# A linear-attention and expert-MLP kernel: numerators in three steps, another order of the first units, and queries rounded by a DMA

## The chip, the core and the metric

The kernel runs on one NeuronCore of a Trainium2 chip. A NeuronCore has five engines that run side by side, each through its own list of instructions in order: TensorE (PE, matrix products into PSUM), VectorE (DVE), ScalarE (ACT), GpSimd (POOL) and SyncE (SP, which here only issues DMAs). They wait for one another by semaphores. The metric is the device time of one execution in microseconds (us).

## The reference

Three stages follow one another, all in float32:

```python
# 1. linear attention, q, k, v: (2, 8, 576, 64), w_phi: (64, 128)
proj = x @ w_phi                                   # for x = q and x = k
proj = proj - max(abs(proj), axis=-1)
phi  = concat([exp(proj), exp(-proj)])             # 256 features
kv   = k_p.T @ v;  z = sum(k_p, axis=seq)
out  = (q_p @ kv) / (q_p @ z + 1e-6)               # numerator / denominator
# 2. x (1152, 512):  x = ((x @ w_a) * (x @ w_b)) @ w_out        # 1536 inner columns
# 3. four experts:   out = sum_e p_e * (relu(x @ w1[e]) @ w2[e])   # 1024 inner columns each
```

## The kernel before

**Split operands.** Most float32 matrix products are made of three products of rounded parts (type fp32r): high by high, high by low, low by high. So each operand has a high part (the value rounded) and a low part (the value minus the high part). `two_parts` makes the pair: a copy with rounding on ScalarE (L84) and a subtraction on another engine, mostly GpSimd (L85). Some products (`kv`, `num`, the transposes `rt`) run in plain float32; the profile counts each of those matmuls twice.

**The attention loop.** The loop over `slot` has 36 items, 18 of keys (slots 0 to 17) and 18 of queries (slots 18 to 35), then ten slots more. An item is 256 columns of k or q: two tiles of 128 tokens by two heads. In a slot:

- `split_x(slot + 3)` makes the two parts `xp` of the item three slots ahead from `xraw`, which holds three items and is loaded by SP (L100);
- `stage_proj(slot)` multiplies six times with w_phi (`pj`, L165 to L167); VectorE takes the maximum (`mx`, L170) and subtracts it (`r`, L172);
- for keys, three slots later, `stage_kv` accumulates `kv` (L199);
- for queries, four slots later, `stage_rt` transposes `r` on TensorE (`rt`, L219) and ScalarE writes the exponentials `qp` (L237);
- when all `qp` of two pairs of heads (a half of a batch; there are four halves) are there, `stage_num` runs in the next slot: three groups of matmuls in a row (denominator, then two numerators, `num`, L265), each into a tile of the pool `nd` with two buffers. ScalarE copies the denominator (`den`, L272), VectorE turns it into reciprocals (L279 to L284) a slot later and multiplies the numerators (`x`, L289), and `stage_xparts` makes the parts `xh` (ScalarE, L295) and `xl` (GpSimd, L296).

`pj`, `rt` and, later, `ab` share the four PSUM buffers of the pool `u`: TensorE can't go on with a new tile before VectorE or ScalarE has read an old one.

**The weights.** The weights of stage 2 are prepared beside this by tasks of a list: `begin` (two ScalarE instructions, `m` and `rn`), `middle` (three VectorE instructions, L369 to L375, one GpSimd addition `wx`, L378, and the next load `raw` by SP) and `parts` (`w`, ScalarE L84 and GpSimd L85). `prep(n)` issues the next n tasks. Before, slots 10 and 14 issue three each, and every slot from 20 on issues one.

**Stage 2.** A unit `unit_ab(j, tp)` treats 256 inner columns for batch `tp` in eight chunks of twelve matmuls (`ab`, L608 to L610); it writes its result `hh` once per four chunks. Its eight products with w_out (`o1`, six matmuls each) go to a queue and run during later units; `free_hh(tp)` runs those of the same batch that are still queued before `hh` is written again. The first unit, (0, 0), is the `fill`: its chunks are issued in the last attention slots, two each in slots 40, 42, 43 and 44 (`FILL`), while batch 1 is still in attention. Then `order` lists the units: (0, 0), (0, 1), (1, 0), (1, 1), (2, 0) and so on.

Of the kernel before, what the change touches and what calls it, by code (L numbers as in the profile page):

```python
# [47 lines left out]
def tile_linear_attention_then_mlps(ctx, tc, qT, kT, v, w_phi, wab, wout, w12, probs, out):  # L48
# [25 lines left out]
    with tc.manual_schedule():  # L74
# [16 lines left out]
        def load_chunk(n):  # L91
# [9 lines left out]
            xraw[n] = t  # L101

        def split_x(i, eng):
            n, c = i // 3, i % 3 * 256
            if c == 0:
                xpart[n] = [r_p.tile([128, NC], F32R, tag=f"xp{k}", name="xp", bufs=2) for k in range(2)]
            hi, lo = (t[:, c:c + 256] for t in xpart[n])
            if i == 0:
                nc.vector.tensor_copy(hi, xraw[n][:, 0:256])
                nc.vector.tensor_tensor(out=lo, in0=xraw[n][:, 0:256], in1=hi.bitcast(F32), op=ALU.subtract)  # L110
# [34 lines left out]
        seq = tiles_of_batch()  # L145
        items = []
        for kind in "kq":
# [10 lines left out]
        def stage_proj(i):  # L158
            kind, b, g, ts_ = items[i]
            ps = u_p.tile([128, 2, 2, 128], F32, tag="u", name="pj")  # L160
            for j in range(2):
                c = i % 3 * 256 + j * 128
                hi, lo = (t[:, c:c + 128] for t in xpart[i // 3])
# [49 lines left out]
        def stage_rt(i):  # L213
# [6 lines left out]
            for t in ts_:  # L220
                for p in ([t[0]] if t[0] != "m" else t[1:]):
                    if (b, p) not in qp_t:
                        qp_t[b, p] = q_p.tile([128, 2, 2, S], F32, tag="qp", name="qp", bufs=3)
            done = []
# [27 lines left out]

        def stage_num(b, half):
            pairs = [(b, 2 * half + k) for k in range(2)]
            qp = [qp_t.pop(bp) for bp in pairs]
            den = q_p.tile([128, 2, HT], F32, tag="den", name="den", bufs=1)
            x = []
            for k in range(3):
                t = nd_p.tile([128, 2, 512], F32, tag="nd", name="num")
                for i in range(2):  # L260
                    for s in range(2):
                        for n in range(4):
                            h = n % 2
                            c = 64 * (1 - h) if k == 0 else 64 * h + 32 * (k - 1)
                            nc.tensor.matmul(  # L265
                                out=t[32 * n:32 * n + 32, i, 0:HT],
                                lhsT=kvz_t[pairs[n // 2]][:, h, s, c:c + 32],
                                rhs=qp[n // 2][:, s, h, HT * i:HT * i + HT],
                                start=(s == 0), stop=(s == 1), tile_position=(0, 32 * n),
                            )  # L270
                if k == 0:
                    nc.scalar.activation(out=den, in_=t[:, :, 0:HT], func=AF.Copy, bias=1e-6)  # L272
                else:
                    x.append(t)
            return x, den

# [471 lines left out]

        NI = len(items)
        NK = NI // 2  # L750
        todo = {}
# [16 lines left out]
        FILL = [NI + 4, NI + 6, NI + 7, NI + 8]  # L768
        fill = unit_ab(0, 0)

        for slot in range(NI + 10):
            if slot < NI:
                kind, b, g, ts_ = items[slot]
                if slot + 3 < NI:
                    split_x(slot + 3, nc.gpsimd)
                stage_proj(slot)
            if slot == NK + 4:
# [11 lines left out]
            if NK <= i < NI:  # L789
                for bb, p in stage_rt(i):  # L790
                    if p % 2:
                        n = slot + (2 if i == NI - 1 else 1)
                        later(n, num, n, bb, p // 2)
            for fn, a in todo.pop(slot, []):
# [6 lines left out]
            if slot == 16:  # L801
                probabilities()
            if slot in FILL:
                for _ in range(2):
                    next(fill)
                    pos[0] += 1
            if slot in (10, 14):
                prep(3)
            if slot >= NK + 2:
                prep(1)  # L810
        assert not todo
# [78 lines left out]
```

## Time and profile before

| | |
|---|---|
| time, median of 3 runs | 735.85 us (735.56 to 736.63) |
| the profiled execution, its own time | 734.41 us |
| its span in the trace | 732.6 us |
| TensorE busy | 711.3 us, 97% |
| VectorE, ScalarE, GpSimd busy | 57%, 42%, 41% |
| share of TensorE in the chain that ended last | 92% |
| mean granted clock of TensorE | 0.998 of full speed |

The profile is of one execution. TensorE is busy nearly everywhere; its idle time is the span less its busy time, 21 us in all. The views by stretches and the waits of TensorE show where these microseconds lie; the share of busy time of the other engines over the whole span says little about the stretches in which TensorE waits for them.

### The profile page before, as it was taken

To read this page: it belongs to the slowest core of one execution; us is meant where nothing else is said; L and a number is where in the kernel's file an instruction comes from. 1 tells how busy PE (TensorE), PEld (TensorE's weight loads), DVE (VectorE), ACT (ScalarE), POOL (GpSimd) and SP (SyncE) were. 2 spreads that over 40 slices of the span, in tenths; PEclk is the share of its full clock that TensorE was granted. 3 is DMA by queue.
4 is the path that set the end of the run, shared out by engine and by line. 5 is a ranking of instruction groups with operands and counts; after the bars stand their busy time and mean duration, and the time that the engine had idled before them with its cause. 6 is when DMAs were issued, how large, how long until landed. Compare 5 with 4: busy or idle time off the path is not lost.

```text
span 732.6 us, 12645 instructions
## 1 busy us (share of the span) xinstructions
PE 711.3 (97%) x4928; PEld 652.1 (89%) x4928; DVE 419.3 (57%) x717; ACT 304.2 (42%) x626; POOL 302.9 (41%) x277
## 2 busy tenths in 40 slices
PE   7998988999999999999899999999999999999998
PEld 7996657999999999999888898988988898989896
DVE  6678796446666575363545555545455545545454
ACT  6566764554535351243553333323233323333221
POOL 3356545444434354312683425344442535343300
PEclk9999999999999999999999999999999999999999
DMA  7534211222323231022041011111111011100003
GB/s 200 148 111 125 58 59 59 82 92 87 91 83 87 78 96 30 1 58 86 2 116 30 30 57 58 30 55 33 58 40 47 30 59 58 30 29 1 1 1 129
DMA packets 49707, 46.25 MB, mean 63 GB/s; under 512 B 8304, under 2 KB 41584, under 8 KB 49648
## 3 DMA queue, kind: packets, MB, share of 16 engines
q1 hardware_dynamic: 49344, 45.26, 21.0%
q8 instruction: 38, 0.62, 0.4%
q10 hardware_dynamic: 304, 0.20, 0.1%
q14 instruction: 21, 0.17, 0.1%
HBM read 43.08 MB, written 2.36 MB: 62 GB/s over the span
## 4 chain that ended last, share of the span: by engine, by line
PE 92%; DVE 3%; ACT 3%; issue 1%; POOL 1%; DMA 0%; DVEq 0%; ACTq 0%; POOLq 0%
PE acc L682 9%; PE acc L681 9%; PE acc L680 9%; PE ab L609 7%; PE ab L610 7%; PE ab L608 7%; PE X L533 5%; PE kv L199 5%; PE X L534 5%; PE X L535 5%; PE acc L639 3%; PE acc L640 3%; PE acc L638 3%; PE num L265 3%; PE Z L534 2%; PE Z L533 2%
## 5 line engine op out<-in xcount | busy, mean ns | idle before, releaser
L696 DVE SCALAR_TENSOR_TENSOR oacc<-acc,pr,oacc 128x512 f32<-128x512 f32 (+1 forms) x136 | 101.4, 746 | 117.2 <-PE acc L682 117.2
L85 POOL TENSOR_TENSOR w<-wx,w 128x512 fp32r<-128x512 f32 x68 | 92.1, 1355 | 154.9 <-ACT w L84 154.9
L609 PE MATMUL ab<-xl,w 128*128 128x288 f32 x384 | 113.3, 295 | 2.0 <-POOL xl L296 2.0
L85 POOL TENSOR_TENSOR wc<-wt,wc 128x512 fp32r<-128x512 f32 (+1 forms) x48 | 69.8, 1483 | 109.4 <-ACT wc L84 109.4
L682 PE MATMUL acc<-w,hhb 128*128 128x512 f32 x288 | 114.1, 396 | 0.9 <-DVE hhb L657 0.9
L608 PE MATMUL ab<-xh,w 128*128 128x288 f32 x384 | 113.5, 296 | 1.2 <-ACT xh L295 1.2
L610 PE MATMUL ab<-xh,w 128*128 128x288 f32 x384 | 113.4, 295 | 0.0
L681 PE MATMUL acc<-w,hhb 128*128 128x512 f32 x288 | 113.1, 393 | 0.0
L680 PE MATMUL acc<-w,hhb 128*128 128x512 f32 x288 | 112.6, 391 | 0.0
L533 PE MATMUL X<-xc,wc 128*128 128x288 f32 x256 | 77.2, 302 | 1.4 <-ACT h L538 1.4
L534 PE MATMUL X<-xc,wc 128*128 128x288 f32 x256 | 75.8, 296 | 0.7 <-DVE xc L85 0.7
L656 ACT ACTIVATE hhb<-h 128x288 fp32r<-128x288 f32 x64 | 36.2, 566 | 96.8 <-DVE h L541 96.7
L535 PE MATMUL X<-xc,wc 128*128 128x288 f32 x256 | 75.4, 295 | 0.0
L609 PEld LDWEIGHTS ab<-xl,w 128*128 128x128 f32 x384 | 72.2, 188 | 2.2 <-POOL xl L296 2.2
L608 PEld LDWEIGHTS ab<-xh,w 128*128 128x128 f32 x384 | 72.2, 188 | 1.9 <-ACT xh L295 1.5
L378 POOL TENSOR_TENSOR wx<-wx,rn 128x512 uint32<-128x512 uint32 x36 | 46.3, 1287 | 63.1 <-DVE wx L375 63.1
L610 PEld LDWEIGHTS ab<-xh,w 128*128 128x128 f32 x384 | 72.2, 188 | 0.0
L538 ACT ACTIVATE h<-X 128x288 f32<-128x288 f32 x64 | 25.9, 405 | 104.5 <-PE X L535 104.5
L682 PEld LDWEIGHTS acc<-w,hhb 128*128 128x128 f32 x288 | 54.0, 188 | 15.6 <-DVE hhb L657 4.4
L657 DVE SCALAR_TENSOR_TENSOR hhb<-h,hhb 128x288 fp32r<-128x288 f32 x64 | 40.5, 633 | 42.2 <-ACT hhb L656 42.2
L681 PEld LDWEIGHTS acc<-w,hhb 128*128 128x128 f32 x288 | 54.0, 188 | 8.4
L680 PEld LDWEIGHTS acc<-w,hhb 128*128 128x128 f32 x288 | 54.1, 188 | 7.7
(99 smaller groups left out, 1605.8 us busy)
## 6 DMA issues: line engine op xcount, KB each, us to landing
raw<-in_wab SPq DMA_DIRECT2D x192, 64.0 KB, 2.0
wt<-in_w SPq DMA_DIRECT2D x64, 128.0 KB, 2.4
wx<-in_w SPq DMA_DIRECT2D x32, 256.0 KB, 2.9
raw<-in_wout SPq DMA_DIRECT2D x12, 512.0 KB, 3.7
xraw<-in_qT SPq DMA_DIRECT2D x6, 384.0 KB, 3.1
out<-oacc SPq DMA_DIRECT2D x8, 256.0 KB, 2.0
xraw<-in_kT SPq DMA_DIRECT2D x5, 384.0 KB, 4.2
v<-in_v SPq DMA_DIRECT2D x8, 192.0 KB, 4.4
```

The lines of the kernel that those rows point to most:

```text
L85: eng.tensor_tensor(out=lo, in0=src, in1=hi.bitcast(F32), op=ALU.subtract)
L378: nc.gpsimd.tensor_tensor(out=x, in0=x, in1=r, op=ALU.add)
L533: nc.tensor.matmul(out=ps, lhsT=whi, rhs=xhi, start=first and a == 0, stop=False, skip_group_check=True)
L534: nc.tensor.matmul(out=ps, lhsT=whi, rhs=xlo, start=False, stop=False, skip_group_check=True)
L535: nc.tensor.matmul(out=ps, lhsT=wlo, rhs=xhi, start=False, stop=a == 1, skip_group_check=True)
L608: nc.tensor.matmul(out=t, lhsT=whi, rhs=hi, start=(c == 0), stop=False)
L609: nc.tensor.matmul(out=t, lhsT=whi, rhs=lo, start=False, stop=False)
L610: nc.tensor.matmul(out=t, lhsT=wlo, rhs=hi, start=False, stop=(c == KD - 1))
L680: nc.tensor.matmul(out=acc, lhsT=hi, rhs=w[:, 0, f], start=f == 0, stop=False)
L681: nc.tensor.matmul(out=acc, lhsT=hi, rhs=w[:, 1, f], start=False, stop=False)
L682: nc.tensor.matmul(out=acc, lhsT=lo, rhs=w[:, 0, f], start=False, stop=f == 1)
L696: nc.vector.scalar_tensor_tensor(out=oc, in0=acc[:, c:c + step], scalar=sc, in1=oc, op0=ALU.mult, op1=ALU.add)
```

## The change

1. **Numerators in three steps.** The denominator's group of matmuls runs in one slot, the first numerator's in the next, the second's in the one after. `qp` gets four buffers instead of three. The last half starts one slot earlier (slot 40, not 41), and the loop has 45 slots, not 46.
2. **Order of the first units.** After (0, 0) comes (1, 0), then (0, 1) and (1, 1). The chunks of the fill stand in slots 38, 39, 40 (one each), 42 (two), 43 (one) and 44 (two).
3. **High parts of the queries by DMA.** `load_hi` lets GpSimd's queue load each query item's 256 columns a second time, straight into the fp32r tile: 18 DMAs, in slots 12 to 29, six slots ahead of their use. `split_x` then makes only the low part, on GpSimd (L124 of the new file). The tiles `xp` now hold one item each, seven buffers for high parts and four for low ones.
4. **Weight tasks.** `PREP` issues one task in each of the slots 5 to 16, in every second slot from 20 to 34, and in the slots 36 to 44.

```diff
+        def load_hi(i):
+            if NK <= i < NI:
+                xpart[i] = part_x(0)
+                c = i % 3 * 256
+                nc.gpsimd.dma_start(out=xpart[i], in_=qT[i // 3 - B * 3][:, c:c + 256])
...
+            raw = xraw[n][:, c:c + 256]
+            hi = xpart[i] if i >= NK else part_x(0)
+            lo = part_x(1)
...
+            elif i < NK:
+                two_parts(hi, lo, raw, eng)
             else:
-                two_parts(hi, lo, xraw[n][:, c:c + 256], eng)
+                eng.tensor_tensor(out=lo, in0=raw, in1=hi.bitcast(F32), op=ALU.subtract)
...
         def num(slot, b, half):
-            later(slot + 1, div, slot + 1, b, half, *stage_num(b, half))
-
-        def div(slot, b, half, x, den):
+            pairs = [(b, 2 * half + k) for k in range(2)]
+            qp = [qp_t.pop(bp) for bp in pairs]
+            kvz = [kvz_t[bp] for bp in pairs]
+            den = stage_den(stage_num(qp, kvz, 0))
+            later(slot + 1, first, slot + 1, b, half, qp, kvz, den)
+
+        def first(slot, b, half, qp, kvz, den):
+            t = stage_num(qp, kvz, 1)
             rb = stage_rc(den)
-            for k in range(2):
-                later(slot + 1 + k, scaled, slot + 1 + k, b, 2 * half + k, x[k], rb)
-
-        def scaled(slot, b, c, t, rb):
-            later(slot + 1, stage_xparts, b, c, stage_x(t, rb))
-
-
-        FILL = [NI + 4, NI + 6, NI + 7, NI + 8]
+            later(slot + 1, second, slot + 1, b, half, qp, kvz, rb, t)
+
+        def second(slot, b, half, qp, kvz, rb, t0):
+            t1 = stage_num(qp, kvz, 2)
+            later(slot + 1, stage_xparts, b, 2 * half, stage_x(t0, rb))
+            later(slot + 1, third, slot + 1, b, half, rb, t1)
+
+        def third(slot, b, half, rb, t1):
+            later(slot + 1, stage_xparts, b, 2 * half + 1, stage_x(t1, rb))
+
+
+        FILL = {NI + 2: 1, NI + 3: 1, NI + 4: 1, NI + 6: 2, NI + 7: 1, NI + 8: 2}
+        PREP = {s: 1 for s in range(5, NK - 1)} | {s: 1 for s in range(NK + 2, NI, 2)} | {s: 1 for s in range(NI, NI + 9)}
...
-        order = [(j, tp) for j in range(FP1 - 2) for tp in range(B)]
+        order = [(0, 0), (1, 0), (0, 1), (1, 1)] + [(j, tp) for j in range(2, FP1 - 2) for tp in range(B)]
```

On TensorE, where the first half of batch 0 is ready, the three groups stood in one piece before (`num`, 48 matmuls, each of which the trace counts twice); `pj` are projections, `rt` transposes:

```order
L219 MATMUL rt<-ident,r 128x128 x4
L265 MATMUL num<-qp,kvz 32x288 x48
L165 MATMUL pj<-wbp,xp 128x256
L166 MATMUL pj<-wbp,xp 128x256
L167 MATMUL pj<-wbp,xp 128x256
```

At the same place now:

```order
L232 MATMUL rt<-ident,r 128x128 x4
L273 MATMUL num<-qp,kvz 32x288 x16
L178 MATMUL pj<-wbp,xp 128x256
L179 MATMUL pj<-wbp,xp 128x256
L180 MATMUL pj<-wbp,xp 128x256
L178 MATMUL pj<-wbp,xp 128x256
L179 MATMUL pj<-wbp,xp 128x256
L180 MATMUL pj<-wbp,xp 128x256
L232 MATMUL rt<-ident,r 128x128 x4
L273 MATMUL num<-qp,kvz 32x288 x16
```

A slot's projections and transposes now stand between two groups of 16.

On GpSimd, at the end of the keys and the start of the queries, the low parts (`xp`) stood among the weight tasks (`w`, `wx`) before:

```order
L85 TENSOR_TENSOR xp<-xraw,xp 128x256 x6
L85 TENSOR_TENSOR w<-wx,w 128x512
L85 TENSOR_TENSOR xp<-xraw,xp 128x256
L378 TENSOR_TENSOR wx<-wx,rn 128x512
L85 TENSOR_TENSOR xp<-xraw,xp 128x256 x2
```

Now (L124 is a query's subtraction, L110 the DMA of a high part):

```order
L85 TENSOR_TENSOR w<-wx,w 128x512
L124 TENSOR_TENSOR xp<-xraw,xp 128x256
L110 DMA xp<-in_qT 128x256
L387 TENSOR_TENSOR wx<-wx,rn 128x512
L124 TENSOR_TENSOR xp<-xraw,xp 128x256
L110 DMA xp<-in_qT 128x256
L124 TENSOR_TENSOR xp<-xraw,xp 128x256
L110 DMA xp<-in_qT 128x256
```

Each of the subtractions in these slots has a DMA behind it in the same queue.

On TensorE, where the fill ends and the next unit begins, numbers tell the tiles apart. Before, `xh_784` was batch 0, `xh_786` batch 1, and the next unit took batch 1 with the same weights `w_565`:

```order
L608 MATMUL ab_1622<-xh_784,w_825 128x288
L609 MATMUL ab_1622<-xl_785,w_825 128x288
L610 MATMUL ab_1622<-xh_784,w_825 128x288
L608 MATMUL ab_1667<-xh_786,w_565 128x288
L609 MATMUL ab_1667<-xl_787,w_565 128x288
L610 MATMUL ab_1667<-xh_786,w_565 128x288
```

Now `xh_844` is batch 0, and the next unit stays with it:

```order
L617 MATMUL ab_1661<-xh_844,w_629 128x288
L618 MATMUL ab_1661<-xl_845,w_629 128x288
L619 MATMUL ab_1661<-xh_844,w_629 128x288
L617 MATMUL ab_1695<-xh_844,w_1410 128x288
L618 MATMUL ab_1695<-xl_845,w_1410 128x288
L619 MATMUL ab_1695<-xh_844,w_1410 128x288
```

The unit behind the fill needs other weights (`w_1410`) and no tile of batch 1.

## Rows read from the trace of the kernel before

**Rows 1.** Stretches: start:end, length, each engine's busy time (x instructions), TensorE's clock, DMA share, GB/s.
```profile
0.00:56.20 56.20, 51.83 (x448) 50.66 (x449) 39.01 (x68) 34.35 (x71) 23.35 (x34) 1.00 0.56 150
56.20:68.20 12.00, 8.72 (x70) 7.56 (x73) 11.30 (x19) 9.99 (x27) 7.00 (x9) 1.00 0.41 126
68.20:80.80 12.60, 11.31 (x136) 7.64 (x136) 9.31 (x16) 7.49 (x20) 6.50 (x8) 1.00 0.33 99
80.80:94.40 13.60, 12.29 (x143) 8.05 (x142) 11.46 (x18) 8.66 (x22) 7.75 (x8) 1.00 0.14 40
94.40:104.00 9.60, 8.30 (x108) 4.17 (x109) 9.27 (x14) 6.19 (x15) 6.76 (x5) 1.00 0.22 64
114.00:128.50 14.50, 11.29 (x83) 10.85 (x83) 8.61 (x13) 5.40 (x10) 6.21 (x5) 1.00 0.12 37
```
**Rows 2.** Waits of TensorE: us in total, times, longest.
```profile
PE rt L219 <- ACT qp L237: 2.9, 2, 1.5
PE ab L609 <- POOL xl L296: 2.0, 1, 2.0
PE ab L608 <- ACT xh L295: 1.2, 1, 1.2
```
**Rows 3.** Stretches of 10 us behind the handover to batch 1.
```profile
130.00:140.00 10.00, 10.00 (x66) 10.00 (x65) 3.35 (x7) 5.38 (x12) 3.51 (x4) 0.83 0.35 105
140.00:150.00 10.00, 10.00 (x78) 10.00 (x77) 5.64 (x10) 5.47 (x12) 5.50 (x4) 1.00 0.29 80
```
**Rows 4.** Timeline of VectorE: start, length, instruction, count, idle time before it.
```profile
58.33 0.42 DVE L369 TENSOR_SCALAR m<-m 128x512 f32<-128x512 f32 x1
...
59.91 0.68 DVE L170 TENSOR_REDUCE mx<-pj 128x4 f32<-128x512 f32 x1
...
61.30 0.68 DVE L170 TENSOR_REDUCE mx<-pj 128x4 f32<-128x512 f32 x1
...
75.10 0.69 DVE L170 TENSOR_REDUCE mx<-pj 128x4 f32<-128x512 f32 x1 [2.96 <-PE pj L167]
...
87.85 0.69 DVE L170 TENSOR_REDUCE mx<-pj 128x4 f32<-128x512 f32 x1 [1.77 <-PE pj L167]
```
**Rows 5.** Timeline of TensorE, numerators.
```profile
68.12 6.03 PE L265 MATMUL num<-qp,kvz 128*32 128x288 f32 x96
...
96.53 1.16 PE L265 MATMUL num<-qp,kvz 128*32 128x288 f32 x12 [0.49 <-ACT qp L237]
97.90 2.15 PE L265 MATMUL num<-qp,kvz 128*32 128x288 f32 x32 [0.21 <-DVE x L289]
```
**Rows 6.** Instructions on the tile xraw: duration in ns, least/median/most, first and last start.
```profile
L84 ACT ACTIVATE xp<-xraw x35: 397/402/495, 3.7 to 85.4; 128x256 fp32r<-128x256 f32 x35
L85 POOL TENSOR_TENSOR xp<-xraw,xp x33: 722/728/968, 6.4 to 88.1; 128x256 fp32r<-128x256 f32 x33
L100 SPq DMA_DIRECT2D xraw<-in_qT x6: 328/337/371, 37.6 to 68.9; - x6
L85 DVE TENSOR_TENSOR xp<-xraw,xp x2: 418/418/419, 4.7 to 5.0; 128x256 fp32r<-128x256 f32 x2
```
**Rows 7.** Timeline of SP's queue: a DMA of v in many pieces.
```profile
9.96 0.61 SPq L133 DMA_DIRECT2D v<-in_v  x1
```
**Rows 8.** Groups by form, GpSimd's weight tasks, 30 to 128.5 us: count, busy us, mean ns.
```profile
L85 POOL TENSOR_TENSOR w<-wx,w 128x512 fp32r<-128x512 f32 x10 | 13.3, 1332 | 8.4 <-ACT w L84 8.4
L378 POOL TENSOR_TENSOR wx<-wx,rn 128x512 uint32<-128x512 uint32 x10 | 12.7, 1275 | 24.2 <-DVE wx L375 24.2
```
**Rows 9.** Page, DMA issues: count, KB each, median us to landing.
```profile
xraw<-in_qT SPq DMA_DIRECT2D x6, 384.0 KB, 3.1
```
**Rows 10.** Timeline of VectorE: one instruction (L372) at two places.
```profile
94.70 0.43 DVE L372 TENSOR_SCALAR m<-m 128x512 uint32<-128x512 uint32 x1
...
127.20 1.50 DVE L372 TENSOR_SCALAR m<-m 128x512 uint32<-128x512 uint32 x1
```
**Rows 11.** Timeline of GpSimd beside the second of these.
```profile
126.84 1.57 POOL L296 TENSOR_TENSOR xl<-x,xh 128x576 fp32r<-128x576 f32 x1
```

More of the change, by code (lines that the diff above doesn't have):

```diff
@@ L101, in load_chunk, with part_x @@
             xraw[n] = t
+        def part_x(k):
+            return r_p.tile([128, 256], F32R, tag=f"xp{k}", name="xp", bufs=7 - 3 * k)
+        def load_hi(i):
[3 more added lines that the diff above has]
+                nc.gpsimd.dma_start(out=xpart[i], in_=qT[i // 3 - B * 3][:, c:c + 256])
         def split_x(i, eng):
             n, c = i // 3, i % 3 * 256
-            if c == 0:
-                xpart[n] = [r_p.tile([128, NC], F32R, tag=f"xp{k}", name="xp", bufs=2) for k in range(2)]
-            hi, lo = (t[:, c:c + 256] for t in xpart[n])
+            raw = xraw[n][:, c:c + 256]
+            hi = xpart[i] if i >= NK else part_x(0)
+            lo = part_x(1)
+            xpart[i] = hi, lo
             if i == 0:
-                nc.vector.tensor_copy(hi, xraw[n][:, 0:256])
-                nc.vector.tensor_tensor(out=lo, in0=xraw[n][:, 0:256], in1=hi.bitcast(F32), op=ALU.subtract)
+                nc.vector.tensor_copy(hi, raw)
+                nc.vector.tensor_tensor(out=lo, in0=raw, in1=hi.bitcast(F32), op=ALU.subtract)
+            elif i < NK:
+                two_parts(hi, lo, raw, eng)
             else:
-                two_parts(hi, lo, xraw[n][:, c:c + 256], eng)
+                eng.tensor_tensor(out=lo, in0=raw, in1=hi.bitcast(F32), op=ALU.subtract)
             if c == 512:
@@ L146, in tile_linear_attention_then_mlps @@
         items = []
+        NI = 2 * B * 9
+        NK = NI // 2
         for kind in "kq":
@@ L161, in stage_proj @@
             for j in range(2):
-                c = i % 3 * 256 + j * 128
-                hi, lo = (t[:, c:c + 128] for t in xpart[i // 3])
+                hi, lo = (t[:, 128 * j:128 * j + 128] for t in xpart[i])
                 o = ps[:, j].rearrange("p h f -> p (h f)")
@@ L222, in stage_rt @@
                     if (b, p) not in qp_t:
-                        qp_t[b, p] = q_p.tile([128, 2, 2, S], F32, tag="qp", name="qp", bufs=3)
+                        qp_t[b, p] = q_p.tile([128, 2, 2, S], F32, tag="qp", name="qp", bufs=4)
             done = []
@@ L251, in tile_linear_attention_then_mlps, with stage_num, stage_den @@
         xc = {}
-        def stage_num(b, half):
-            pairs = [(b, 2 * half + k) for k in range(2)]
-            qp = [qp_t.pop(bp) for bp in pairs]
-            den = q_p.tile([128, 2, HT], F32, tag="den", name="den", bufs=1)
[L257 to L275, printed above, removed]
+        def stage_num(qp, kvz, k):
+            t = nd_p.tile([128, 2, 512], F32, tag="nd", name="num")
+            for i in range(2):
+                for s in range(2):
+                    for n in range(4):
+                        h = n % 2
+                        c = 64 * (1 - h) if k == 0 else 64 * h + 32 * (k - 1)
+                        nc.tensor.matmul(
+                            out=t[32 * n:32 * n + 32, i, 0:HT],
+                            lhsT=kvz[n // 2][:, h, s, c:c + 32],
+                            rhs=qp[n // 2][:, s, h, HT * i:HT * i + HT],
+                            start=(s == 0), stop=(s == 1), tile_position=(0, 32 * n),
+                        )
+            return t
+        def stage_den(t):
+            den = q_p.tile([128, 2, HT], F32, tag="den", name="den", bufs=1)
+            nc.scalar.activation(out=den, in_=t[:, :, 0:HT], func=AF.Copy, bias=1e-6)
+            return den
         def stage_rc(den):
@@ L756, in num @@
         def num(slot, b, half):
[L757 to L768 removed]
+            pairs = [(b, 2 * half + k) for k in range(2)]
[5 more added lines that the diff above has]
+            t = stage_num(qp, kvz, 1)
+            rb = stage_rc(den)
+            later(slot + 1, second, slot + 1, b, half, qp, kvz, rb, t)
[7 more added lines that the diff above has]
+        PREP = {s: 1 for s in range(5, NK - 1)} | {s: 1 for s in range(NK + 2, NI, 2)} | {s: 1 for s in range(NI, NI + 9)}
         fill = unit_ab(0, 0)
[L771 removed]
+        for slot in range(NI + 9):
             if slot < NI:
@@ L775, in tile_linear_attention_then_mlps @@
                     split_x(slot + 3, nc.gpsimd)
+                load_hi(slot + 6)
                 stage_proj(slot)
@@ L791, in tile_linear_attention_then_mlps @@
                     if p % 2:
-                        n = slot + (2 if i == NI - 1 else 1)
-                        later(n, num, n, bb, p // 2)
+                        later(slot + 1, num, slot + 1, bb, p // 2)
             for fn, a in todo.pop(slot, []):
@@ L802, in tile_linear_attention_then_mlps @@
                 probabilities()
[L803 to L810, printed above, removed]
+            for _ in range(FILL.get(slot, 0)):
+                next(fill)
+                pos[0] += 1
+            prep(PREP.get(slot, 0))
         assert not todo
```

2 lines of the change are left out of this document (removed).

## The prediction, made before the changed kernel ran

> **What bounds the kernel now.** I read the table of stretches first, cut where TensorE's idle time begins and ends. Up to 56.2 us TensorE is busy 51.8 us; the 4.4 us that are missing are the start, before its first matmul. From there to 128.5 us it lacks 3.28, 1.29, 1.31 and 1.30 us in the four stretches of the queries and 3.21 us in the last one [rows 1]: 10.4 us together. The list of TensorE's waits says for whom: in the first of these stretches a transpose waits 2.9 us for ScalarE's `qp`, and in the last one the first unit of batch 1 waits 1.2 us for `xh` and 2.0 us for `xl` [rows 2]. Behind that last wait the clock falls for a while: the stretch from 130 to 140 us has a mean grant of 0.83, between the levels of 1.2 and 2.4 GHz, and holds 66 matmuls where the next one, at 1.00, holds 78 [rows 3]. Twelve matmuls at 10.0/78 = 0.128 us are 1.5 us. So 11.9 us are all that this change can give; the rest of the span is matmuls, whose number stays the same.
>
> The timeline of VectorE then tells why the queries stall. Where nothing else is between, one item's maximum and subtraction take it 61.30 - 59.91 = 1.39 us [rows 4]; it is busy 11.30 of 12.0 us in the first stretch, ScalarE 9.99 [rows 1], and TensorE can be no more than two slots ahead, since its PSUM buffers come free only through these two. Later the picture turns: while TensorE runs the 96 numerator records in one piece, 6.03 us [rows 5], VectorE sits idle for 2.96 us, and at the next such piece for 1.77 us [rows 4]; afterwards TensorE waits for the work that they could have done meanwhile. So this phase loses by taking turns.
>
> **The change, part by part.**
>
> *Weight tasks.* In the first query stretch stood two `middle` tasks; with every second slot, one stands there. It takes VectorE 59.91 - 58.33 = 1.58 us [rows 4]. VectorE is the fuller engine there, so TensorE gains 1.6 us of its 3.28. The tasks taken out go into the slots 5 to 16, where TensorE never waits and VectorE, ScalarE and GpSimd have 17, 22 and 33 us to spare [rows 1]; that hides them, and if it did not, six more tasks (two `middle` of 1.6 us on VectorE) would cost 3 us at most. Their `raw` loads move ahead in SP's queue too, past one load of `xraw`; that tile is used three to six slots later, so I count nothing.
>
> *High parts by DMA.* ScalarE loses 18 copies of 0.40 us [rows 6], 7.2 us in the stretches where `qp` is late; this is part of the gain of the first and the next item, and earns nothing by itself. GpSimd gets 18 DMA issues. No row shows a DMA issued by GpSimd. From below, SP issues a load of these same queries in 0.34 us [rows 6]; from above I take the dearest GpSimd instruction that I found in these stretches, 1.57 us [rows 11]. SP needs 0.61 us for a DMA of many small pieces [rows 7], and GpSimd takes 728 ns for the subtraction that VectorE does in 418 [rows 6]; 0.61 x 728/418 = 1.06 us, so I estimate 1.0 us, as software has to write the pieces one by one. An issue price d decides like this. From slot 12 until the low part that slot 26 needs, GpSimd has 12 issues, 12 subtractions of 0.73 us, two `w` of 1.33 and three `wx` of 1.28 us [rows 6, 8]: 15.2 us + 12 d. TensorE takes nine slots of 51.8/21 = 2.47 us and five of 10.4/6.5 = 1.6 us for it, 30.2 us. So d up to 1.25 us is hidden, and beyond it each issue costs the excess, 18 times in all. What is queued behind an issue is the next subtraction, then the weight tasks, and TensorE's `pj` waits for the subtraction alone. At 1.0 us GpSimd is nearly full, and I set 0.5 us for places where it is late; the ends are 0 at 0.34 us and 18 x (1.57 - 1.25) = 5.8 us. The landing is no bound: SP's query loads land after 3.1 us at three times the size [rows 9], and a subtraction comes three slots, 4.8 us, after its DMA.
>
> A second thing speaks against GpSimd's queue. The same VectorE instruction took 0.43 us alone and 1.50 us beside a subtraction of GpSimd [rows 10, 11]. Four `middle` tasks (two such instructions each) and one reciprocal copy meet the 18 issues; at 1.1 us each that is up to 10 us on VectorE, but five of the nine lie among the queries: 5.4 us at most. I take it as covered by the 0.5 us, since VectorE's 0.43 us will mostly fall between two issues, and keep the 5.4 us as the upper end. The Trainium skill ("SBUF — State Buffer", Who interferes with whom) states that VectorE's two-port modes and GpSimd share one port pair that is locked for a whole instruction, and that descriptors of GpSimd's DMAs can't be written meanwhile. The trace agrees with the lock, 0.43 against 1.50 us; that it holds up DMA issues is not shown by any run yet. By this rule the sum would be up to 5 us worse. The Trainium skill ("DMA: Bandwidth & Descriptors", Specifications) gives about 1 us to the first byte of such a DMA; if all of it held the queue, 18 issues would still be hidden by the bound above.
>
> *Numerators in three steps.* Pieces of 2 us leave VectorE and ScalarE nothing to sit out, so the 1.29, 1.31 and 1.30 us of the three later stretches should mostly go. What stays: the first step of a half still comes right behind the exponentials of its last item; one such wait was 0.49 us [rows 5], and at three halves some 0.4 us each remain. I count 3.9 - 1.3 = 2.6 us gained; the ends are 0 and 3.9. Against it, TensorE enters the numerators 11 times, not 4. A third of the long piece is 6.03/3 = 2.01 us, a single step took 2.15 [rows 5]: 7 x 0.14 = 1.0 us lost.
>
> *Order of the first units.* Behind the fill now stands a unit of batch 0. It brings eight chunks of 12 matmuls, 12.3 us, and the eight queued `o1` are run in its middle, 48 more, 6.1 us. Before, the parts of batch 1 came 3.2 us too late behind the fill; now they have 18 us more. The 3.2 us go whole. I expect no late successor: the weights of unit (1, 0) are tasks 21 to 30 of the list, 29 are issued in the loop and the rest by the second chunk. Units (0, 1) and (1, 1) free the buffers for the weights of j = 2 one unit later than before, and one unit with its `o1` (some 18 us) is left for these six tasks of `w`; at 1.33 + 1.28 us on GpSimd that is 16 us, which just fits. With the wait the fall of the clock goes: 1.5 us.
>
> **The sum.** -1.6 (weight tasks) - 2.6 (steps) - 3.2 (handover) - 1.5 (clock) + 1.0 (entries) + 0.5 (GpSimd late) = -7.4 us. The profiled execution's own 734.41 us become 727.0. The median of the runs is 735.85, 1.44 us above it; the same gain there gives 728.4 us.
>
> **The rivals.**
> - *The query phase stays as it is.* If VectorE's 1.39 us per item, the reciprocals and the `middle` tasks bind however TensorE's pieces lie (it was busy 11.46 of 13.60 us in the third stretch and 9.27 of 9.60 in the fourth, rows that speak for it; its idle 2.96 and 1.77 us speak against it), only the handover is gained: -3.2 - 1.5 + 1.0 = -3.7, 732.1 us.
> - *All idle time goes* and neither entries nor issues cost anything: -11.9, 724.0 us. The full VectorE of the first stretch speaks against it.
> - *GpSimd's queue becomes the bound.* An issue of 1.25 to 1.7 us eats 0 to 7.9 us; the time lies between 728 and 735.9. From 1.25 + 7.9/18 = 1.69 us on the change loses, and beyond 1.77 us by over 0.2%. At 2.0 us it is 13.5 - 7.9 = +5.6: 741.4 us. For it speaks that nothing in the trace bounds a software issue from above and that the lock adds to it; against it, that 1.57 us of GpSimd's time do a 128x576 subtraction, much more than writing some 256 short records.
> - *The change of order starves the units of weights* (the 16 us of 18): the handover's gain is given back once, about 3 us: 731.5 us.
>
> **How the numbers follow.** The forecast and what lies near it (724.5 to 731) has 0.66, a query phase that stays 0.14, GpSimd's queue between 1.25 and 1.7 us 0.08, beyond it 0.08, weights 0.04. What a measurement of this kernel can tell from no change is about 0.2%, 1.5 us. Faster by more: 0.66 + 0.14 + 0.04 + half of the middle GpSimd case = 0.88, which I lower to 0.86, since an unseen kind of DMA may bring a cost outside the span; same 0.06; slower 0.08. The range reaches from near the full removal, 724.5 us, to 734, which takes in the upper bound of the issue, -7.9 + 5.8 = -2.1 (733.8); the slow rival is left out.
>
> **What would show it.** TensorE's idle time between 56 and about 122 us is 3 to 4 us, most of it before the first numerator and on `qp`; no wait on `xl` or `xh` longer than 0.3 us; a clock of 1.00 in all stretches; VectorE has no idle place over 1.5 us among the queries. The first `o1` stands in the middle of the second unit. GpSimd's issues among the queries take 0.7 to 1.3 us, and TensorE waits for `xp` by less than 1 us in all. The prediction is wrong if `pj` waits for `xp` by several us (GpSimd's queue), if the `qp` and `r` waits stay at 7 us (the phase was bound by work, not by turns), or if a wait on `w` appears in the units (1, 0) or (2, 0).

## The result, and the profile after

| | before | after |
|---|---|---|
| time, median of 4 runs | 735.70 us (735.11 to 736.63) | 727.00 us (725.65 to 728.59) |
| the profiled execution, its own time | 734.41 us | 725.65 us |
| its span | 732.6 us | 723.5 us |
| TensorE busy | 711.3 us | 709.0 us |
| mean granted clock | 0.998 | 0.999 |

The changed kernel takes 0.9881 of the time of before [0.9853, 0.9910], 8.7 us less in the medians, against a forecast of 7.4 us less. 727.0 us lies inside the range, 1.4 us under the forecast of 728.4.

First the stretches of the kernel after, cut at the same times as [rows 1], with one more behind the fill. The columns are those of [rows 1].

```profile
56.20:68.20 12.00, 9.47 (x79) 7.63 (x81) 11.34 (x19) 7.99 (x21) 7.85 (x13) 1.00 0.50 122
68.20:80.80 12.60, 12.60 (x160) 8.00 (x152) 10.61 (x18) 6.48 (x16) 8.63 (x11) 1.00 0.55 141
80.80:94.40 13.60, 13.59 (x164) 8.82 (x164) 11.64 (x18) 9.91 (x25) 6.77 (x7) 1.00 0.01 2
94.40:104.00 9.60, 9.60 (x120) 6.40 (x112) 6.25 (x11) 6.81 (x17) 5.86 (x5) 1.00 0.34 95
114.00:128.50 14.50, 14.50 (x111) 14.50 (x111) 8.19 (x12) 9.30 (x18) 7.94 (x6) 1.00 0.17 51
128.50:145.00 16.50, 16.05 (x121) 15.82 (x120) 9.93 (x14) 7.43 (x15) 5.22 (x4) 1.00 0.30 84
```

TensorE's idle time in the four query stretches goes from 3.28, 1.29, 1.31 and 1.30 us [rows 1] to 2.53, 0.00, 0.01 and 0.00; at the handover to batch 1 it goes from 3.21 to 0, and a new 0.45 us stands in the last row. Together 10.39 become 2.99: 7.4 us less. The clock is 1.00 in all these rows, where it was 0.83 for 10 us [rows 3], which had cost 1.5 us by the prediction's count. 7.4 + 1.5 = 8.9, against the 9.1 us by which the span is shorter. The totals of the table divide these 9.1 us a little differently: idle time falls by 6.8 us (21.3 to 14.5) and busy time by 2.3. So 0.6 us of idle time came anew outside these rows, nearly all of it at the end of the kernel, and 0.8 us of the shorter busy time is not explained.

The waits of TensorE in the kernel after, between 56 and 145 us (total, times, longest):

```profile
PE rt L232 <- ACT qp L250: 2.1, 4, 0.7
PE acc L648 <- DVE hhb L630: 0.4, 1, 0.4
PE pj L178 <- DVE r L185: 0.2, 1, 0.2
PE pj L180 <- POOL xp L124: 0.2, 1, 0.2
```

The waits on `xl` and `xh` of [rows 2] are gone. The one of `rt` on `qp` was 2.9 us in two pieces and is now 2.1 us in four. Before, there were also these, and three shorter waits of the numerators:

```profile
PE pj L165 <- ACT qp L237: 1.9, 3, 1.3
PE rt L219 <- DVE r L172: 0.9, 1, 0.9
```

None of these is left. `pj` waits for a low part, the thing that would have shown a full GpSimd queue, once, for 0.2 us.

No row of before could tell anything of DMAs issued by GpSimd. Here is their group in the view of the tile `xp` of the kernel after (duration in ns, least/median/most, first and last start):

```profile
L110 POOL DMA_DIRECT2D xp<-in_qT x18: 567/567/697, 38.1 to 77.8; - x18
```

and a line of its page's DMA issues (KB each, median us to landing):

```profile
xp<-in_qT POOLq DMA_DIRECT2D x18, 128.0 KB, 3.3
```

An issue holds GpSimd's queue for 0.567 us, between SP's 0.34 [rows 6] and the 1.0 us of the estimate, far under the 1.25 us from which it was to cost anything.

TensorE's timeline at the first half's numerators, to be read against the single piece of 6.03 us in [rows 5] (start, length, instruction, count, idle time before it):

```profile
66.83 0.66 PE L232 MATMUL rt<-ident,r 128*128 128x128 f32 x4 [0.48 <-ACT qp L250]
67.42 2.15 PE L273 MATMUL num<-qp,kvz 128*32 128x288 f32 x32
69.49 0.39 PE L178 MATMUL pj<-wbp,xp 128*128 128x256 f32 x1
...
70.31 0.60 PE L232 MATMUL rt<-ident,r 128*128 128x128 f32 x4
70.84 2.15 PE L273 MATMUL num<-qp,kvz 128*32 128x288 f32 x32
```

The pieces are 2.15 us long, with a slot's projections and transposes between them. VectorE now sits idle 1.60 us before the first maximum behind such a piece, where it was 2.96 [rows 4]:

```profile
70.51 0.69 DVE L183 TENSOR_REDUCE mx<-pj 128x4 f32<-128x512 f32 x1 [1.60 <-PE pj L180]
```

### The profile page after: what moved, and what is told of

Read it like the earlier page. It is cut to its first block, busy times and chain, and to the rows that moved or that the text cites. A ratio compares the mean times of both kernels' runs of the same rounds, so it can differ in the third digit from the quotient of the medians.

```text
span 723.5 us, 12684 instructions
## 1 busy us (share of the span) xinstructions
PE 709.0 (98%) x4928; PEld 649.6 (90%) x4928; DVE 425.0 (59%) x717; ACT 298.9 (41%) x608; POOL 312.8 (43%) x295
## 4 chain that ended last, share of the span: by engine, by line
PE 95%; DVE 2%; ACT 1%; issue 1%; DMA 1%; POOL 0%; DVEq 0%; SPq 0%; POOLq 0%; ACTq 0%
PE acc L691 9%; PE acc L690 9%; PE acc L689 9%; PE ab L617 7%; PE ab L619 7%; PE ab L618 7%; PE X L542 5%; PE kv L212 5%; PE X L543 5%; PE X L544 5%; PE acc L648 4%; PE num L273 3%; PE acc L649 3%; PE acc L647 3%; PE Z L542 2%; PE Z L543 2%
## 5 line engine op out<-in xcount | busy, mean ns | idle before, releaser
L85 POOL TENSOR_TENSOR w<-wx,w 128x512 fp32r<-128x512 f32 x68 | 90.6, 1334 | 142.4 <-ACT w L84 142.3
```

The costliest lines, as they stand in the source:

```text
L85: eng.tensor_tensor(out=lo, in0=src, in1=hi.bitcast(F32), op=ALU.subtract)
```

## The experiments

Medians and ratios are against runs of the kernel before on the same chip, beside the experiment. "The changed kernel" is the one above.

### Each part taken out of the changed kernel

**The same kernel again** (no edit).

> The changed kernel once more, as a control. Its four runs lay at two levels: 725.7 us at a mean clock of 0.999 (span 723.5) and 728.3 us at 0.996 (span 726.1 to 726.5). Theory: in some executions the clock falls once more, for some us, in or behind the first query stretch, where TensorE still waits often; so about half of the runs lie at 728, with a clock of 0.996, and none between. Rival: the levels belong to the moment or to the chip; then these runs all lie at one level.

Measured: 727.64 us (725.71 to 728.59), ratio 0.9879 [0.9864, 0.9894]. The five spans are 723.6, 724.9, 725.5, 725.6 and 726.5 us at clocks of 0.998 to 1.000. There are values between the ends, and no fixed relation to the clock, so the idea of two levels doesn't hold; a spread of 3 us belongs to this kernel. In this profile and the first one the clock is 1.00 in all query stretches; where it fell in profiles of kernels that are as fast as this one, that was at stage 3's start (last section), not among the queries. So single runs of the others are read with that spread in mind.

**Numerators whole, all else as changed.**

```diff
             den = stage_den(stage_num(qp, kvz, 0))
-            later(slot + 1, first, slot + 1, b, half, qp, kvz, den)
+            x = [stage_num(qp, kvz, k) for k in (1, 2)]
+            later(slot + 1, div, slot + 1, b, half, x, den)
...
```

> The changed kernel, with the three groups of numerator matmuls in one piece again (the DMAs, the order of units and the weight tasks stay). Theory, taking turns: VectorE and ScalarE sit idle during 6 us pieces and TensorE waits for them afterwards, so 2.5 to 3.9 us of TensorE's idle time come back between 68 and 104 us, with VectorE idle places of 1.5 to 3 us, and the span goes from 723.5 to 726 to 727.4. Rival, relief: the waits went because weight tasks and copies were taken out of the query slots, and the pieces do not matter; then the span stays within 1 us of 723.5 and TensorE's idle time after 68 us stays under 1 us.

Measured: 731.61 us (730.0 to 734.35), ratio 0.9958 [0.9944, 0.9973]. The loss is larger than expected. The profile is of the slowest of its seven executions (734.35 us, mean clock 0.991); the one at a clock of 1.000 took 730.0 us, 4.3 us more than the fastest of the changed kernel. The stretches of this kernel:

```profile
68.20:80.80 12.60, 11.34 (x136) 7.63 (x136) 6.81 (x13) 5.14 (x13) 5.37 (x8) 1.00 0.42 109
80.80:94.40 13.60, 12.00 (x122) 6.83 (x123) 6.97 (x12) 5.87 (x13) 7.19 (x9) 0.75 0.19 49
94.40:104.00 9.60, 8.18 (x104) 4.54 (x106) 9.36 (x15) 7.09 (x18) 4.16 (x4) 1.00 0.03 10
```

and VectorE's timeline in it, the two places where it was idle for more than a microsecond between 66 and 100 us:

```profile
75.09 0.69 DVE L183 TENSOR_REDUCE mx<-pj 128x4 f32<-128x512 f32 x1 [5.50 <-PE pj L180]
...
92.11 0.69 DVE L183 TENSOR_REDUCE mx<-pj 128x4 f32<-128x512 f32 x1 [6.46 <-PE pj L180]
```

This is the turn-taking in its plainest form: while TensorE runs a whole piece, VectorE waits 5.5 and 6.5 us for projections (the second time beside a piece that the fallen clock made longer); in these three stretches TensorE lacks 1.26, 1.60 and 1.42 us, 4.3 us together, as much as the execution at full clock lost. VectorE is idle for longer than before (2.96 us, [rows 4]), with fewer weight tasks in these slots, so the stall doesn't come from too much work. The clock of 0.75 in the second row follows a wait too. On TensorE's timeline of this kernel a numerator waits 2.57 us for `x`, and the 96 records behind it take 8.76 us, not the 6.03 of [rows 5]:

```profile
82.40 8.76 PE L273 MATMUL num<-qp,kvz 128*32 128x288 f32 x96 [2.57 <-DVE x L298]
```

**The old order of units.**

```diff
-        order = [(0, 0), (1, 0), (0, 1), (1, 1)] + [(j, tp) for j in range(2, FP1 - 2) for tp in range(B)]
+        order = [(j, tp) for j in range(FP1 - 2) for tp in range(B)]
```

> The changed kernel with the units in the old order (0, 0), (0, 1), (1, 0). Theory, handover: the last low part of batch 1 is done at 119.9 us in the changed kernel and the fill's last chunk ends at 118.0, so TensorE waits 2 to 3 us for xh and xl there again, and the clock may fall once more for 1.5 us: span 725.5 to 728. Rival: batch 1 now starts one slot earlier, which alone is enough, so no wait over 0.5 us and a span of 723.5 to 724.

Measured: 726.89 us (726.03 to 727.92), ratio 0.9885 [0.9871, 0.9899]: no difference from the changed kernel. Of the wait that should have come back, this much is left in TensorE's list of waits (total, times, longest):

```profile
PE ab L618 <- POOL xl L305: 0.3, 1, 0.3
```

It was 2.0 us, with 1.2 on `xh` before it [rows 2]. With the other edits, batch 1 is ready in time for the old order too. The rival was right about the wait; its span of 723.5 to 724 us was met by one execution of four (724.0 to 725.9), a spread like that of the changed kernel itself.

**The high parts by ScalarE, no GpSimd DMAs.**

```diff
         def load_hi(i):
-            if NK <= i < NI:
+            if False:
...
-            hi = xpart[i] if i >= NK else part_x(0)
+            hi = part_x(0)
...
-            elif i < NK:
+            elif True:
                 two_parts(hi, lo, raw, eng)
```

> The changed kernel with the high parts of the queries made by ScalarE again (18 copies of 0.40 us, no DMA on GpSimd's queue, the tiles xp as in the changed kernel). Theory: VectorE is the fuller engine in the first query stretch and the pieces did the rest, so the DMAs are worth little by themselves: 0 to 1.5 us, span 723.5 to 725. Rival, ScalarE is what qp waits for: 2.5 us or more, span 726 and above, with the waits of rt on qp at 4 us or more. Against both: without issues on GpSimd the low parts come earlier, and the span falls below 723.3.

Measured: 725.25 us (724.92 to 728.0), ratio 0.9875 [0.9859, 0.9890]. The DMAs are worth nothing that can be measured. Without them the wait on `qp` is longer (3.2 us in five pieces, after 2.1) and the one of `pj` on GpSimd (0.2 us) is gone; in all TensorE waits 0.7 us more between 56 and 145 us, which does not show in the time.

**The old table of weight tasks.**

```diff
-        PREP = {s: 1 for s in range(5, NK - 1)} | {s: 1 for s in range(NK + 2, NI, 2)} | {s: 1 for s in range(NI, NI + 9)}
+        PREP = {10: 3, 14: 3} | {s: 1 for s in range(NK + 2, NI + 9)}
```

> The changed kernel with weight tasks issued as before (three in slots 10 and 14, one in every slot from 20). Theory: a second middle of 1.6 us on VectorE comes back into the first query stretch and two more later, TensorE waits 1.6 us more before 68 us and up to 1.5 us more after it: span 725 to 727. Rival: VectorE has room, since the pieces let it work through; span 723.5 to 724.3.

Measured: 730.79 us (729.33 to 734.46), ratio 0.9950 [0.9932, 0.9968], outside what was expected. The loss is not in the first query stretch, where TensorE was busy 9.24 us (9.47 after), but in the next two:

```profile
68.20:80.80 12.60, 12.09 (x140) 7.96 (x140) 12.18 (x16) 7.94 (x21) 11.23 (x15) 1.00 0.63 166
80.80:94.40 13.60, 10.71 (x119) 6.17 (x121) 13.17 (x21) 7.57 (x18) 8.49 (x8) 0.87 0.21 53
```

The longest of TensorE's waits among the queries of this kernel:

```profile
PE rt L232 <- DVE r L185: 3.6, 2, 2.9
```

With numerators in steps and a task in every slot from 20 on, VectorE is full (12.18 of 12.60, 13.17 of 13.60 us), and a transpose waits 2.9 us for `r`. So the steps bring their gain only where VectorE has room.

### Parts alone, on the kernel before or beside one other

**The order alone, on the kernel before.**

```diff
-        order = [(j, tp) for j in range(FP1 - 2) for tp in range(B)]
+        order = [(0, 0), (1, 0), (0, 1), (1, 1)] + [(j, tp) for j in range(2, FP1 - 2) for tp in range(B)]
```

> The kernel before with nothing but the new order of the first units, (0, 0), (1, 0), (0, 1), (1, 1). Theory: the 3.2 us of waits on xh and xl and the 1.5 us of low clock behind them go: span 732.6 - 4.7 = 727.9, or down to 729 if a wait on weights of some tenths comes. Rival: another wait takes its place (the weights of unit (1, 0), or PSUM), and the span stays above 731.

Measured: 732.78 us (730.46 to 734.78), ratio 0.9952 [0.9934, 0.9970]. The handover's waits on `xh` and `xl` go, and part comes back later; TensorE's wait between 110 and 145 us of its trace:

```profile
PE acc L638 <- ACT part L538: 1.1, 1, 1.1
```

There are 0.4 us more on `hhb`, at 167 us: 1.5 of the 3.2 us in all. Five of its six spans (728.7 to 733.0 us) lie above the 727.9 to 729 that were expected.

**Steps and tasks, no DMAs, the old order.** The earlier last half and the fill's new places stay, here and in the next kernel.

```diff
-            if NK <= i < NI:
+            if False:
...
-        order = [(0, 0), (1, 0), (0, 1), (1, 1)] + [(j, tp) for j in range(2, FP1 - 2) for tp in range(B)]
+        order = [(j, tp) for j in range(FP1 - 2) for tp in range(B)]
```

> The changed kernel without two of its parts: the high parts of the queries are made by ScalarE, and the units stand in the old order; left are the three steps, the new slots of the fill and the weight tasks. Taken out one by one, neither part cost anything measurable. Theory, the steps and the tasks carry it all, since batch 1 is ready earlier through them: 725 to 727.5 us, a wait on xl of 0.3 to 1 us, span 723.5 to 726. Rival, the two parts stand in for each other (one of them must be there): a wait of 2 us or more comes back, 728.5 us and above.

Measured: 725.66 us (724.21 to 726.96), ratio 0.9859 [0.9845, 0.9874]. The whole gain is here. Its interval overlaps that of the changed kernel, so it can't be called faster; it does as well with 18 DMAs and one order fewer.

**Tasks alone**: the same, with the numerators whole.

```diff
-            later(slot + 1, first, slot + 1, b, half, qp, kvz, den)
+            x = [stage_num(qp, kvz, k) for k in (1, 2)]
+            later(slot + 1, div, slot + 1, b, half, x, den)
...
```

> As the run with steps and tasks alone, but with the numerators in one piece: of the change only the weight tasks and the fill's slots are left. Theory, without the steps TensorE waits as in the kernel before in the three later query stretches (3 to 4.5 us), and batch 1 comes late again: 730 to 734 us. Rival, the tasks are the whole gain: 727 us.

Measured: 731.01 us (729.2 to 732.95), ratio 0.9938 [0.9925, 0.9952]. Against the run before it, beside the same runs of before, the steps are worth 731.01 - 725.66 = 5.35 us. What they take away is seen in its stretches, 10.62 of 12.60, 12.45 of 13.60 (at a clock of 0.87) and 8.58 of 9.60 us, and in TensorE's waits:

```profile
PE num L273 <- DVE x L298: 2.3, 1, 2.3
...
PE ab L618 <- POOL xl L305: 0.3, 1, 0.3
```

The second line tells of the handover: with the old order and whole numerators it is cured all the same, by what is left of the change here, the table of tasks, the earlier last half and the fill's new places. These three were not tried apart.

### From where on a GpSimd issue costs time

**Two DMAs of 128 columns per item, then four of 64.** (The edit for four; for two, 4 is 2.)

```diff
-                nc.gpsimd.dma_start(out=xpart[i], in_=qT[i // 3 - B * 3][:, c:c + 256])
+                w = 256 // 4
+                for d in range(4):
+                    nc.gpsimd.dma_start(out=xpart[i][:, d * w:d * w + w], in_=qT[i // 3 - B * 3][:, c + d * w:c + d * w + w])
```

> The changed kernel with every high part loaded by two DMAs of 128 columns: 36 issues. An issue took 0.57 us, so two take 1.13 us per item, under the 1.25 us that I worked out as hidden. Theory: waits of pj on xp grow by at most 1 us, span 723.5 to 725. Rival, the bound is nearer: 18 x 0.57 = 10 us come on a GpSimd that is already late, and the span grows by 4 us or more.

> The changed kernel with every high part loaded by four DMAs of 64 columns: 72 issues, 4 x 0.57 = 2.27 us per item. Theory of the slow rival: beyond 1.25 us each item costs the excess, 18 x 1.0 = 18 us of waits of pj on xp, less some of TensorE's other waits (2 to 3 us): span 737 to 742, slower than the kernel before. Rival: an issue's time goes by the bytes, not by the DMA, so four take some 1 us and the span stays under 726.

Measured: 726.71 us (725.51 to 731.37), ratio 0.9879 [0.9855, 0.9903], for two, and 741.25 us (740.28 to 741.63), ratio 1.0065 [1.0052, 1.0078], for four. The issues of the second kernel on `xp`:

```profile
L112 POOL DMA_DIRECT2D xp<-in_qT x72: 537/557/702, 38.3 to 97.5; - x72
```

A quarter of the columns costs the same 0.56 us, so an item's price d is about 1.1 us for two and 2.2 us for four. At 1.1 GpSimd was busy 10.85 of 12.0 us and nothing was lost. At 2.2 the stretches are these:

```profile
56.20:68.20 12.00, 7.76 (x49) 6.75 (x48) 10.21 (x13) 2.62 (x5) 12.00 (x22) 0.80 0.60 110
68.20:80.80 12.60, 8.13 (x38) 7.31 (x38) 6.40 (x10) 5.28 (x15) 12.60 (x21) 0.64 0.57 110
80.80:94.40 13.60, 13.60 (x150) 8.21 (x152) 9.51 (x16) 5.77 (x15) 13.60 (x23) 0.89 0.51 90
```

and the largest of TensorE's waits is this:

```profile
PE pj L182 <- POOL xp L126: 10.7, 8, 2.0
```

GpSimd never rests in these stretches, TensorE waits eight times for a low part, and its mean clock is between the levels of 1.2 and 2.4 GHz in all three. This is the prediction's slow rival, with its mechanism and its place. The runs with two and four DMAs show that the cost begins between 1.1 and 2.2 us. An estimate within that: 741.25 - 727.64 = 13.6 us over 18 items is 0.76 us per item, so it begins at about 2.2 - 0.8 = 1.4 us; the prediction had 1.25. The estimate counts what the fallen clock cost as part of the price, and supposes that each item pays the same.

The same kernel shows what can happen where VectorE and a DMA issue meet. On VectorE's timeline, one instruction at two places:

```profile
65.12 1.47 DVE L383 TENSOR_SCALAR m<-m 128x512 uint32<-128x512 uint32 x1
...
90.01 0.43 DVE L383 TENSOR_SCALAR m<-m 128x512 uint32<-128x512 uint32 x1
```

and on GpSimd's beside them:

```profile
64.70 2.17 POOL L112 DMA_DIRECT2D xp<-in_qT  x4
...
88.95 2.21 POOL L112 DMA_DIRECT2D xp<-in_qT  x4
```

GpSimd did nothing but issue from 64.70 to 66.87 us, at 0.54 us each, as ever; VectorE's instruction took 1.47 us for its usual 0.43. It isn't so each time: at 90.01 us, with issues running from 88.95 to 91.16, it took 0.43 us. What tells the two apart stays open. The Trainium skill ("SBUF — State Buffer", Who interferes with whom) says that the two share a port pair by an exclusive lock and that the issue order decides who blocks. The trace agrees at the first of the two places, 0.43 against 1.47 us, where VectorE lost; none of the 72 issues took over 0.70 us.

### An attempt at the 2.5 us that remain

**Weight tasks in the slots 17 and 18 too, then none before slot 28, and the last `kvz` copy on ScalarE**: on the changed kernel, then without the DMAs. The loop issues 28 tasks, not 29.

```diff
-                nc.vector.tensor_copy(t, kv_ps.pop((b, p))[:, 0])
+                if (b, p) == (B - 1, NP - 1):
+                    nc.scalar.activation(out=t, in_=kv_ps.pop((b, p))[:, 0], func=AF.Copy)
+                else:
+                    nc.vector.tensor_copy(t, kv_ps.pop((b, p))[:, 0])
...
-        PREP = {s: 1 for s in range(5, NK - 1)} | {s: 1 for s in range(NK + 2, NI, 2)} | {s: 1 for s in range(NI, NI + 9)}
+        PREP = {s: 1 for s in range(5, NK + 1)} | {s: 1 for s in (28, 30, 32, 34, 35)} | {s: 1 for s in range(NI, NI + 9)}
```

> The changed kernel with two things more, to take VectorE's load out of the first query stretch, in which TensorE still waits 2.5 us: weight tasks in the slots 5 to 18, 28, 30, 32, 34, 35 and 36 to 44 (no middle of 1.6 us between slots 19 and 31), and the last copy of kv (0.7 us) on ScalarE. Theory, VectorE binds there: TensorE's idle time from 56 to 68 us falls from 2.5 to under 1 us, span 721.8 to 722.5, time 724 us at full clock. Rival, the turn-taking of TensorE and ScalarE over the four PSUM buffers binds: idle time stays above 2 us and the span at 723.5.

> The same two things, with the high parts of the queries made by ScalarE. Theory: ScalarE has room once the pieces are short, so it is as fast as the run with DMAs, span 721.5 to 723. Rival: ScalarE, with the copy of kv and six copies of 0.40 us more in the first query stretch, is now what TensorE waits for, span 724 and above.

Measured: 726.93 us (726.77 to 728.2), ratio 0.9881 [0.9868, 0.9894], and 726.0 us (725.71 to 726.64), ratio 0.9866 [0.9853, 0.9878]. Neither gains. In the first of them TensorE is busy 8.97 us of the 12.0 in the first query stretch, less than the 9.47 after, and the wait has a new owner on TensorE's timeline:

```profile
59.15 0.39 PE L180 MATMUL pj<-wbp,xp 128*128 128x256 f32 x1 [1.43 <-POOL xp L124]
```

GpSimd's timeline before that:

```profile
54.12 1.51 POOL L85 TENSOR_TENSOR w<-wx,w 128x512 fp32r<-128x512 f32 x1 [3.22 <-ACT w L84]
55.60 0.90 POOL L124 TENSOR_TENSOR xp<-xraw,xp 128x256 fp32r<-128x256 f32 x1
56.45 0.57 POOL L110 DMA_DIRECT2D xp<-in_qT  x1
57.14 1.27 POOL L390 TENSOR_TENSOR wx<-wx,rn 128x512 uint32<-128x512 uint32 x1
58.38 0.72 POOL L124 TENSOR_TENSOR xp<-xraw,xp 128x256 fp32r<-128x256 f32 x1
```

The low part for which `pj` waits until 59.15 us stands behind a `wx` of 1.27 us and the `w` before it. Without the DMAs it is the same picture (1.60 us). Moving the tasks out of VectorE's full stretch put them in front of GpSimd's most urgent work. The waits of `rt` on `qp` did shrink, from 2.1 us to 1.6 and 1.0, though VectorE stayed as full there as before (11.16 and 11.46 us of 12.0).

## Why the prediction was right, and where it was off

The direction, the mechanism of each large term and the range held. By its own steps, each term against the trace:

| term | predicted, us | in the trace after, us |
|---|---|---|
| weight tasks, first query stretch | -1.6 | 3.28 to 2.53: -0.75 |
| steps, the three later stretches | -2.6 | 3.90 to 0.01: -3.9 |
| handover | -3.2 | 3.21 to 0, new wait 0.45: -2.8 |
| clock behind it | -1.5 | 1.00 throughout: -1.5 |
| eleven entries into the numerators | +1.0 | 0 |
| GpSimd late | +0.5 | 0.2, within the first line |
| sum | -7.4 | -8.9 |

**Bounds.** That TensorE's idle time between 56 and 128.5 us, and the clock behind it, was all there was to gain held: 8.9 us are found there, against a span that is 9.1 us shorter. Three of the signs that it named came out otherwise: TensorE's idle time there is 2.5 us and not 3 to 4, an issue takes 0.57 us and not 0.7 to 1.3, and VectorE has an idle place of 1.60 us where none over 1.5 was to be.

**Steps: mis-sized.** The term kept back 1.3 us for waits in front of a half's first step, from a wait of 0.49 us [rows 5]. After, no numerator waits (0.0 in the group row of the next paragraph); only the transposes ahead of the first half's first step do (0.48 us, in the first stretch), and the three later stretches lack nothing. The reason given, turns and not work, is shown by the whole numerators with fewer tasks: VectorE idle 5.5 and 6.5 us, TensorE short of 4.3 us all the same. What the trace of before couldn't show is the price of losing them now: 5.35 us, since a wait of 2.3 to 2.6 us appears at the second half and the clock falls behind it.

**Entries: too dear, and counted against a piece that wasn't there.** The 0.14 us came from one step of 2.15 us against a third of 6.03. By groups, the numerators' records of the kernel before, between 56.2 and 128.5 us (count, busy us, mean ns, idle before):

```profile
L265 PE MATMUL num<-qp,kvz 128*32 128x288 f32 x384 | 25.8, 408 | 1.3 <-ACT den L272 0.6 <-ACT qp L237 0.5 <-DVE x L289 0.2
```

and of the kernel after:

```profile
L273 PE MATMUL num<-qp,kvz 128*32 128x288 f32 x384 | 25.6, 409 | 0.0
```

The same 384 records are busy for the same time. Before, they did not stand in four pieces: the third half came in rows of 20, 12, 32 and 32 records, two of which [rows 5] shows. And the price is smaller, since a timeline's row includes the modelled end of the last matmul, which the next one covers. What follows the whole piece at 68.12 us is this:

```profile
74.08 0.39 PE L165 MATMUL pj<-wbp,xp 128*128 128x256 f32 x1
```

So a third of it is 5.96/3 = 1.99 us, and a step, from 67.42 to the start of its neighbour at 69.49, is 2.07: 0.08 us for an entry.

**Weight tasks: mis-sized, and not a term of its own.** Its stretch gained 0.75 us, half of the 1.58 us taken from VectorE, and the tasks can't claim even that: with the old table TensorE was busy 9.24 us there, 0.23 less than after, and the changed kernel's second profile had 9.30. VectorE is still busy 11.34 of the 12.0 us. What TensorE waits for there now are its transposes, in the kernel after (timeline):

```profile
58.87 0.66 PE L232 MATMUL rt<-ident,r 128*128 128x128 f32 x4 [0.52 <-ACT qp L250]
...
60.70 0.66 PE L232 MATMUL rt<-ident,r 128*128 128x128 f32 x4 [0.42 <-ACT qp L250]
...
62.78 0.66 PE L232 MATMUL rt<-ident,r 128*128 128x128 f32 x4 [0.72 <-ACT qp L250]
```

and ScalarE's exponentials beside them:

```profile
59.56 1.08 ACT L250 ACTIVATE qp<-rt 128x512 f32<-128x512 f32 x2 [0.74 <-PE rt L232]
61.39 1.34 ACT L250 ACTIVATE qp<-rt 128x128 f32<-128x128 f32 x6 [0.75 <-PE rt L232]
```

ScalarE starts as a transpose ends and takes 1.08 us; the next transpose starts as it ends: 60.70 - 58.87 = 1.83 us for one round, in which ScalarE itself waits 0.74 us. It is a round trip, not a full ScalarE (7.99 of 12.0 us), which would also explain why copies taken from ScalarE earned nothing. That the four shared buffers of `pj` and `rt` make the round is my reading of the order in which they are used; no run changed their number. The rival, that VectorE's full list in this stretch sets the pace, is not excluded: both attempts to empty it ended in GpSimd's wait. On the other hand, the old tasks cost the changed kernel 0.71% (0.9950 against 0.9879, some 5 us), not 1.6 us: the steps need the room on VectorE. The sum treated both as independent and so missed the interplay. That it came within 1.5 us is in part luck: the weight tasks and the handover were set too high by 0.9 and 0.4 us, the steps too low by 1.3, and entries and late GpSimd charged with 1.5 us that did not come.

**Handover: right in size, the cause shared.** The new order cures it (alone it gave 0.9952), but the old order with the rest of the change cures it as well, down to a wait of 0.3 us. The prediction credited the order alone and overlooked that its other edits bring batch 1 earlier. Its fear for the weights of (1, 0) and (2, 0) has no row: no wait on `w` stands in the list.

**GpSimd's queue: right.** The estimate of 1.0 us was too high by 0.43. The threshold of 1.25 us lies where the runs with two and four DMAs leave it, between 1.1 and 2.2, and near the estimate of 1.4; the slot of 10.4/6.5 us in its working stands in no row, however. The contention with VectorE, 5.4 us at most, cost nothing among the queries as long as the changed kernel issued its DMAs: VectorE's instruction of [rows 10] fell twice there, at 61.01 and 74.57 us, took 0.43 us each time, and GpSimd stood idle beside it.

What stays open: the 3 us by which equal kernels differ from run to run, and what bounds the remaining 2.5 us of the first query stretch, since both attempts turned into GpSimd's wait.

## What to carry to other kernels

Where two engines feed each other through a few shared buffers, a long piece on one makes the other idle, and the idle time comes back as a wait later: read the helper's idle places on its timeline, not its busy share, and split the piece. Before adding up gains, ask which term makes room for which; here steps and tasks were worth 5 us each in the presence of the other, and two of four edits nothing measurable beside them. Price a software DMA of this kind (64 to 256 columns of 128 rows) by its count, not by its size, and compare the count with the room left in the issuing engine's queue up to the next thing that somebody waits for.

## What the runs showed that was not expected

- An issue on GpSimd's queue takes 0.567 us for 128 rows of 256 columns, 0.55 for 128 and 0.557 for 64 columns; landing takes 3.3, 2.7 and 2.7 us.
- The clock can fall or not behind the same waits. Near 350 us, where stage 2 hands over to stage 3, the changed kernel and the one with the old order have the same two longest waits (1.4 us for `h`, 0.7 us for `xc`) and the same busy time, and only the second lost the clock. The stretch of 5 us, in the kernel after:

```profile
350.00:355.00 5.00, 3.61 (x27) 3.53 (x27) 2.18 (x3) 4.59 (x10) 2.83 (x2) 1.00 0.00 0
```

  and with the old order of units:

```profile
350.00:355.00 5.00, 3.60 (x16) 3.37 (x16) 1.73 (x2) 3.92 (x7) 2.45 (x2) 0.67 0.00 0
```

  27 records against 16: part of the spread between runs lies here. With steps and tasks the two runs at a clock of 1.0 had spans of 722.4 and 723.1 us, the two at 0.997 and 0.998 had 724.7 and 725.2. It doesn't explain all of the spread: the changed kernel once had 725.6 us at a clock of 1.0.
